# Twenty products instead of 24 for one half of one group's w_in product, and an earlier place for that half's weight sums

## The chip, the cores and the metric

The kernel runs on one core of a Trainium2 chip. The metric is the device time of one execution in microseconds (us), lower is better. A median of three runs is given for the kernel before. Engine names are those of the profile: PE is the matrix engine, PEld its weight load, DVE the vector engine, ACT the scalar engine, POOL the general engine, SP the engine that issues most transfers.

## The reference: what is computed

Two blocks follow each other. The first is a gated linear attention over 4 batches, 8 heads, 768 positions and a head width of 48. The second is a two-layer network on its result, laid out as 3072 rows of 384 numbers.

```
state = alpha[t] * state + outer(k[t], v[t])     # 48 x 48 for every batch and head
y[t]  = q[t] @ state
x = y as (batch * position, head * width)        # 3072 x 384
h = x @ w_in                                     # w_in 384 x 2048
g = h / (1 + exp(-h))                            # silu
out = g @ w_out                                  # w_out 2048 x 384
```

All of it is in 32-bit floating point; `w_in` and `w_out` come in as 64-bit numbers and are converted on the chip.

## The kernel before, in words

`quotients` is the function that runs; `general`, a slower fallback, stands behind a flag and isn't run on these inputs.

**Attention.** The 3072 rows are 24 chunks of 128 rows (`NT`, line 402). A chunk's attention is spread over two steps of the main loop (line 1185), each step with four slots. `products` (line 698) and `quotient` (line 742) are DVE work: transposes of alpha, k and q, two scans, and the products kp (lines 737 and 739) and p (line 758). In the next step come `scores` (line 780: PE multiplies p by kp, ACT copies the result, POOL masks it), `values` (line 831: PE, then an ACT copy into `xt`) and `states` (line 853: PE, and a DVE addition at line 868). `flip` (line 760) turns kp for the state by way of memory. So PE cannot start the scores of a chunk before DVE has written that chunk's p.

**Network.** Four chunks are a group, so there are 6 groups; a group has two halves of 256 rows. `enter_plain` (line 897) computes `x @ w_in` for one half of the rows and eight of the sixteen 128-column blocks of `w_in` (a `pair`), in four pieces; a piece is six matrix products of 128x256 on PE, and one silu on ACT. `enter` (line 917) computes the same for both halves of the rows together with a scheme of fast matrix multiplication: 20 products in seven pieces, where the plain way takes 24 for the same outputs. Each product is two matrix products of 128x256 (line 929). The scheme needs sums of blocks of `w_in` (`sums_w`, line 589, 23 DVE operations for a pair, from the table at line 335), sums of blocks of the rows (`sums_x`, line 878, 11 DVE operations, line 343), and for each call 12 ACT copies out of PSUM (line 936), 13 DVE additions or subtractions (line 944), one more at line 998, and four silus (line 941) that follow those additions. `sums_w` writes some of its results over `w_in` itself, so no plain product may use that pair of columns afterwards. `leave` (line 1021) computes `g @ w_out` for half a group, with seven products in seven pieces (a scheme of the same kind), and DVE additions at lines 1033, 1042, 1074, 1076 and 1085. `side_by_side` (line 1016) is one DVE addition that `leave` needs.

**Which groups use which.** Group 0 and group 1 are computed by `enter_plain`; groups 2 to 5 by `enter`. The sums of `w_in` for pair 0 are made during `leave(0, 1)`, those for pair 1 during `leave(1, 0)` (line 1050, function `done`).

**Order.** The pieces of the network stand in one list, `pieces` (line 1120), each with a weight of 12 and with the number of chunks that must have been through `values` before it. `both` (line 1116) takes two lists alternately. `fill` (line 1166) is called at the end of every slot and takes so many pieces as are due: within a phase (`phases`, line 1125; `marks`, line 1152) the work is spread evenly over the slots. The second phase, the one with group 1's later parts, runs from slot 35 to slot 50, four slots to a step. Its list before is

```
pieces += [plain(1, 1, 0)] * 4
both([(leave(0, 1), 12, GB)] * 7, [plain(1, 0, 1)] * 4 + [plain(1, 1, 1)] * 4)
```

PE's instructions keep the order in which the program traces them once `late` is filled (`settle`, line 1154, at slot 31). DVE's order is made by the framework's list scheduler when the program is built, apart from the sums (lines 582 to 587), which keep their order among themselves (line 594). [...]

`late` holds the buffers that are allocated at slot 31 over the space of the start-up buffers: `wx` for the sums of `w_in`, `xc` for the sums of rows (one buffer, line 879), `part` (one buffer) for `enter`, `turn` (one buffer) for the transposed k and q.

Of the kernel before, what the change touches and what calls it, by code (L numbers as in the profile page):

```python
# [355 lines left out]
def quotients(  # L356
# [22 lines left out]
    late = {}  # L379
# [25 lines left out]
    GB = 4  # L405
# [183 lines left out]
    def sums_w(pair, upto):  # L589

        r = slice(2 * pair, 2 * pair + 2)
        while sums_done[pair] < min(upto, len(SUMS_W)):
            to, sa, a, sb, b = SUMS_W[sums_done[pair]]
            tc.keep_in_program_order(
                combine(block_w(to)[:, r], sa, block_w(a)[:, r], sb, block_w(b)[:, r]))
            sums_done[pair] += 1

    sums_done = [0] * (NQ // 2)

    def differences(i):  # L600

        if i < HF // 2:
            i = slice(2 * i, 2 * i + 2)
            tc.keep_in_program_order(
                dve.tensor_tensor(t1[:, i], b12[:, i], b11[:, i], ALU.subtract))
            dve.tensor_tensor(t2[:, i], b22[:, i], t1[:, i], ALU.subtract)
            dve.tensor_tensor(t4[:, i], b21[:, i], t2[:, i], ALU.subtract)
        else:
            i -= HF // 2
            side_by_side(0, i % 2, i // 2)  # L610
            i = slice(2 * i, 2 * i + 2)
            dve.tensor_tensor(b12[:, i], b22[:, i], b12[:, i], ALU.subtract)
# [275 lines left out]
    def g_tiles(grp, pair):  # L888
        for h in range(2):
            gts[grp, h, pair] = gpool.tile([128, 4, 2, TB], F32, name="g")  # L890
# [6 lines left out]
    def enter_plain(grp, h, pair):  # L897

        if h == 0:
            g_tiles(grp, pair)  # L900
        xt = xts[2 * grp + h]
        for f in range(8 * pair, 8 * pair + 8, 2):
            ps = bank(f // 2 % 3).rearrange("p (e n) -> p e n", e=2)
            for e in range(2):
                for t in range(NKT):
                    pe.matmul(ps[:, e, :], lhsT=w_in[:, t, (f + e) * 128 : (f + e + 1) * 128],
                              rhs=xt[:, t, :], start=(t == 0), stop=(t == NKT - 1))
            q, i = divmod(f, 4)
            act.activation(gts[grp, h, pair][:, i : i + 2, q % 2, :], ps, AF.Silu)  # L909
            if grp == 1 and pair == h == 0:  # L910
                differences(f // 2)
                differences(4 + f // 2)
            if grp > 0 and f % 8 == 6:
                side_by_side(grp, h, pair)
            yield

    def enter(grp, pair):
        g_tiles(grp, pair)
        halves = [gts[grp, h, pair] for h in range(2)]

        s = [halves[o % 2][:, o // 2] for o in range(8)]
        todo = iter(PRODUCTS)

        def new(i):
            return bank(i).rearrange("p (e n) -> p e n", e=2)

        def add(ps, first=False):
            w, x = next(todo)
            for e in range(2):
                pe.matmul(ps[:, e], lhsT=block_w(w)[:, 2 * pair + e], rhs=block_x(grp, x),  # L930
                          start=(first and e == 0), stop=(e == 1), skip_group_check=True)

        def copy(ps, to=None):
            if to is None:
                to = late["part"].tile([128, 2, TB], F32, name="part")
            act.copy(to, ps)  # L936
            return to

        def silu(h, i):
            x = halves[h][:, i : i + 2]  # L940
            act.activation(x, x, AF.Silu)  # L941

        def tt(to, a, b, op=ALU.add):
            dve.tensor_tensor(to, a, b, op)  # L944

        a, b, c = [new(i) for i in range(3)]
        add(a, True)
        copy(a, s[6])
        add(b, True)
        copy(b, s[2])  # L950
        add(c, True)
        tt(s[6], s[6], copy(c), ALU.subtract)
        yield
        add(a)
        t = copy(a)
        add(b)
        copy(b, s[4])
        add(c)
        copy(c, s[7])
        tt(s[7], s[7], t, ALU.subtract)  # L960
        yield
        add(a)
        copy(a, s[5])
        add(b)
        copy(b, s[3])
        tt(s[5], s[5], s[3])
        add(c)
        copy(c, s[0])
        yield
        add(a)  # L970
        tt(s[4], a, s[4])
        b = new(1)
        add(b, True)
        add(b)
        copy(b, s[1])
        yield
        c = new(2)
        add(c, True)
        tt(s[2], s[2], copy(c), ALU.subtract)
        a = new(0)  # L980
        add(a, True)
        tt(s[6], a, s[6])
        silu(0, 2)
        add(b)
        tt(s[5], copy(b), s[5], ALU.subtract)
        yield
        add(c)
        tt(s[1], c, s[1])
        tt(s[3], s[1], s[3], ALU.subtract)
        a = new(0)  # L990
        add(a, True)
        tt(s[2], a, s[2])
        add(b)
        tt(s[7], b, s[7])
        silu(1, 2)
        yield
        add(c)
        combine(s[1], -1, s[1], -1, s[0])
        tt(s[0], c, s[0])
        silu(0, 0)  # L1000
        a = new(0)
        add(a, True)
        tt(s[3], a, s[3])
        silu(1, 0)
        turn.append(turn.pop(0))
        for h in range(2):
            side_by_side(grp, h, pair)
        yield
# [12 lines left out]
    def leave(grp, h):  # L1021


        def product(ps, m, k, w, first=False):
            for i in range(HF):
                q = i // 2
                x = gts[grp, h, q // 2][:, 2 * (i % 2) + k, q % 2, m * C : (m + 1) * C]
                pe.matmul(ps, lhsT=x, rhs=w[:, i], start=(first and i == 0), stop=(i == HF - 1),
                          skip_group_check=True)

        def subtract(to, x, y):
            for pair in range(NQ // 2):
                dve.tensor_tensor(cells(grp, h, pair, *to), cells(grp, h, pair, *x),  # L1033
                                  cells(grp, h, pair, *y), ALU.subtract)

        def store(m, c, x, y=None):
            ci, b = divmod(GB * grp + 2 * h + m, B)
            o = opool.tile([128, HO], F32, name="o")
            if y is None:
                act.copy(o, x)  # L1040
            else:
                dve.tensor_tensor(o, x, y, ALU.add)  # L1042
            r = b * S + ci * C

            (gps if grp < NG - 1 else nc.sync).dma_start(out[r : r + C, c * HO : (c + 1) * HO], o)  # L1045

        u1, u2, u3, u4 = [rpool.tile([128, HO], F32, name=f"u{j}") for j in range(4)]
        steps = iter(range(7))

        def done():  # L1050
            if 2 * grp + h in (1, 2):
                sums_w(2 * grp + h - 1, 4 * next(steps) + 4)

        def new(i):
            return out_bank(i, HO)

        a, b = new(0), new(1)
        product(a, 0, 0, b11, True)
        act.copy(u1, a)
        subtract((0, 0), (1, 0), (0, 0))  # L1060
        done()
        yield
        product(b, 1, 0, t1, True)
        act.copy(u4, b)  # L1064
        done()
        yield
        product(a, 0, 1, b21)
        store(0, 0, a)
        subtract((0, 1), (0, 1), (0, 0))
        done()  # L1070
        yield
        b = new(1)
        product(b, 0, 0, t2, True)
        dve.tensor_tensor(u2, b, u1, ALU.add)
        subtract((1, 0), (1, 1), (0, 0))
        dve.tensor_tensor(u2, u2, u4, ALU.add)
        done()
        yield
        a = new(0)
        product(a, 0, 1, b22, True)  # L1080
        store(0, 1, a, u2)
        done()
        yield
        product(b, 1, 0, b12)
        dve.tensor_tensor(u3, b, u1, ALU.add)
        store(1, 1, u3, u4)
        done()
        yield
        a = new(0)
        product(a, 1, 1, t4, True)  # L1090
        store(1, 0, a, u3)
        done()
        yield
# [13 lines left out]
    def plain(grp, h, pair):  # L1107
        return (enter_plain(grp, h, pair), 12, 2 * (2 * grp + h) + 2)

    def group(grp):  # L1110
        return [[(enter(grp, pair), 12, GB * grp + GB)] * 7 for pair in range(2)]

    def output(grp):
        return [[(leave(grp, h), 12, GB * grp + GB)] * 7 for h in range(2)]
# [1 line left out]
    def both(x, y):  # L1116
        for i in range(max(len(x), len(y))):
            pieces.extend(x[i : i + 1] + y[i : i + 1])

    pieces = []  # L1120
# [3 lines left out]
    pieces += [plain(1, 0, 0)] * 4 + [(leave(0, 0), 12, GB)] * 7  # L1124
    phases = [len(pieces)]
    pieces += [plain(1, 1, 0)] * 4
    both([(leave(0, 1), 12, GB)] * 7, [plain(1, 0, 1)] * 4 + [plain(1, 1, 1)] * 4)
    phases.append(len(pieces))
    before = output(1)
    for grp in range(2, NG):  # L1130
# [168 lines left out]
```

## Time and profile before

| what | value |
|---|---|
| median of 3 runs | 561.26 us (560.49 to 562.18) |
| span of the profiled execution, first to last instruction | 558.1 us |
| median less span (what lies around it) | 3.2 us |
| PE busy | 541.4 us, 97% of the span |
| PEld busy | 488.8 us, 88% |
| DVE busy | 445.1 us, 80% |
| ACT busy | 208.4 us, 37% |
| POOL busy | 75.9 us, 14% |
| mean granted PE clock | 0.994 |

For the profiled execution only its span is given, and no device time of its own, so what lies around the span is taken from the median of the runs. A row of a timeline gives the start, the time from the first start to the last end of the instructions it merges, the engine, the line, the output and the inputs, and a number of instructions; a bracket gives the idle time of the engine ahead of it and what ended it. A matrix product in 32 bits appears as two MATMUL records. Matrix products overlap in PE's pipeline, so the distance between starts, not the length of one record, is what each costs on PE.

### The profile page before, as it was taken

To read this page: it belongs to the slowest core of one execution; us is meant where nothing else is said; L and a number is where in the kernel's file an instruction comes from. 1 tells how busy PE (TensorE), PEld (TensorE's weight loads), DVE (VectorE), ACT (ScalarE), POOL (GpSimd) and SP (SyncE) were. 2 spreads that over 40 slices of the span, in tenths; PEclk is the share of its full clock that TensorE was granted. 3 is DMA by queue.
4 is the path that set the end of the run, shared out by engine and by line. 5 is a ranking of instruction groups with operands and counts; after the bars stand their busy time and mean duration, and the time that the engine had idled before them with its cause. 6 is when DMAs were issued, how large, how long until landed. Compare 5 with 4: busy or idle time off the path is not lost. (4 is left out here: it accounts for less than half of the span.)

```text
span 558.1 us, 12640 instructions
## 1 busy us (share of the span) xinstructions
PE 541.4 (97%) x5026; PEld 488.8 (88%) x5026; DVE 445.1 (80%) x801; ACT 208.4 (37%) x466; POOL 75.9 (14%) x146
## 2 busy tenths in 40 slices
PE   5999999999999999999999999999999999999996
PEld 3788887998899898899999999988998999998996
DVE  5887889974999799997998986998894775857531
ACT  3456643223333243353353353353263341432200
POOL 4100010221211211021021021021121000001000
PEclk9799999999999999999999999999999999999999
DMA  9999861164445525355445654717712122333101
GB/s 218 255 276 177 232 189 40 38 164 108 126 131 136 142 62 134 88 145 157 129 109 142 194 141 115 198 22 179 180 48 84 53 99 95 111 109 106 38 25 32
DMA packets 99220, 70.13 MB, mean 126 GB/s; under 512 B 56272, under 2 KB 88656, under 8 KB 99152
## 3 DMA queue, kind: packets, MB, share of 16 engines
q1 hardware_dynamic: 97232, 65.30, 44.6%
q0 software_dynamic: 1920, 3.93, 2.0%
q8 instruction: 41, 0.67, 0.5%
q14 instruction: 27, 0.22, 0.1%
HBM read 61.34 MB, written 7.86 MB: 124 GB/s over the span
## 5 line engine op out<-in xcount | busy, mean ns | idle before, releaser
L388 PE MATMUL ps_o<-w_out,g 128*128 128x192 f32 x768 | 134.7, 329 | 1.1 <-DVE o L1042 0.9
L388 PEld LDWEIGHTS ps_o<-w_out,g 128*128 128x128 f32 x768 | 125.4, 190 | 5.1 <-DVE o L1042 2.3
L388 PE MATMUL ps_m<-xt,w_in 128*128 128x256 f32 x480 | 113.6, 383 | 1.5 <-ACT xt L851 1.1
L388 PEld LDWEIGHTS ps_m<-xt,w_in 128*128 128x128 f32 x480 | 89.1, 190 | 14.4 <-ACT xt L851 1.6
L388 PE MATMUL ps_o<-wt,g 128*128 128x192 f32 x576 | 99.7, 326 | 0.0
L388 PEld LDWEIGHTS ps_o<-wt,g 128*128 128x128 f32 x576 | 95.1, 190 | 1.6 <-issue 0.2
L388 PE MATMUL ps_m<-xc,w_in 128*128 128x256 f32 x288 | 70.7, 382 | 0.0
L685 DVE TENSOR_REDUCE seen<-bits 128x1 f32<-128x384 int32 (+2 forms) x65 | 42.5, 689 | 24.0 <-DMA bits<-in_moe_w_out_dram 19.6
L388 PEld LDWEIGHTS ps_m<-xc,w_in 128*128 128x128 f32 x288 | 53.6, 190 | 7.0 <-DVE g L944 0.3
L941 ACT ACTIVATE g<-g 128x1024 f32<-128x1024 f32 x32 | 33.0, 1056 | 59.0 <-DVE g L944 59.0
L1033 DVE TENSOR_TENSOR g<-g 128x512 f32<-128x512 f32 x72 | 49.8, 708 | 6.1 <-PE ps_o L388 6.1
L1045 POOL DMA_DIRECT2D out_dram<-o x40 | 22.0, 550 | 223.2 <-DVE o L1042 127.6
L813 POOL TENSOR_SCALAR_AFFINE_SELECT g<-g 64x256 f32<-64x256 f32 x64 | 34.2, 534 | 124.8 <-ACT g L806 105.8
L388 PE MATMUL ps_m<-xc,wx 128*128 128x256 f32 x192 | 50.0, 383 | 1.0 <-DVE xc L586 1.0
L936 ACT COPY g<-ps_m 128x512 f32<-128x512 f32 x64 | 36.5, 588 | 36.5 <-PE ps_m L388 36.4
L388 PEld LDWEIGHTS ps_m<-xc,wx 128*128 128x128 f32 x192 | 35.2, 190 | 5.3 <-ACT u L1064 1.3
L944 DVE TENSOR_TENSOR g<-ps_m,g 128x512 f32<-128x512 f32 x56 | 37.0, 684 | 2.9 <-PE ps_m L388 2.7
L722 DVE TENSOR_TENSOR_SCAN u<-al,one 128x516 f32<-128x516 f32 x24 | 30.0, 1249 | 10.6 <-ACT al L719 10.3
L909 ACT ACTIVATE g<-ps_m 128x512 f32<-128x512 f32 x32 | 19.1, 596 | 42.8 <-PE ps_m L388 42.3
L936 ACT COPY part<-ps_m 128x512 f32<-128x512 f32 x32 | 18.9, 589 | 43.0 <-DVE g L944 21.3
L752 DVE TENSOR_TENSOR_SCAN p<-al,inv 128x516 f32<-128x516 f32 x24 | 29.9, 1246 | 1.0 <-PE ps_a L388 0.4
L388 PE MATMUL ps_a<-g,vn 128*32 128x128 f32 x768 | 27.5, 278 | 1.8 <-POOL g L801 1.7
(126 smaller groups left out, 611.4 us busy)
## 6 DMA issues: line engine op xcount, KB each, us to landing
bits<-in_moe_w_in_dram SPq DMA_DIRECT2D x24, 512.0 KB, 4.8
bits<-in_moe_w_out_dram SPq DMA_DIRECT2D x32, 384.0 KB, 3.1
at<-in_alpha_dram SPq DMA_DIRECT2D x64, 96.0 KB, 2.5
kt<-in_k_dram SPq DMA_DIRECT2D x64, 96.0 KB, 2.5
qt<-in_q_dram SPq DMA_DIRECT2D x64, 96.0 KB, 2.6
bits<-in_alpha_dram SPq DMA_DIRECT2D x9, 512.0 KB, 3.8
out_dram<-o POOLq DMA_DIRECT2D x40, 96.0 KB, 2.4
flips<-turn SPq DMA_DIRECT2D x12, 256.0 KB, 2.4
```

The source lines that it names most:

```text
L388: in_order(nc.tensor.matmul(*args, **kw))
L685: dve.tensor_reduce(seen[kind][which][:, i : i + 1], x, axis=AX, op=op, apply_absolute_value=True))
L722: dve.tensor_tensor_scan(u[:, end - 1 :: -1], sg[:, end:0:-1], one[:, end:0:-1], 0.0, ALU.mult, ALU.add)
L752: dve.tensor_tensor_scan(p[:, 0:end], sg[:, 0:end], iv[:, 0:end], 0.0, ALU.mult, ALU.add)
L813: gps.affine_select(x, x, pattern=[[0, NP], [1, CH]], compare_op=ALU.is_ge, fill=0.0, base=0, channel_multiplier=-1)
L909: act.activation(gts[grp, h, pair][:, i : i + 2, q % 2, :], ps, AF.Silu)
L936: act.copy(to, ps)
L941: act.activation(x, x, AF.Silu)
L944: dve.tensor_tensor(to, a, b, op)
L1033: dve.tensor_tensor(cells(grp, h, pair, *to), cells(grp, h, pair, *x), cells(grp, h, pair, *y), ALU.subtract)
L1045: (gps if grp < NG - 1 else nc.sync).dma_start(out[r : r + C, c * HO : (c + 1) * HO], o)
```

## The change

Group 1's second pair of columns no longer goes through `enter_plain` for each half (two times four pieces) but through one `enter(1, 1)` (seven pieces, `second(1, 1)`). Its sums of the rows, `sums_x(1)`, are put ahead of it in the list, after the four pieces of `plain(1, 1, 0)`. The sums of `w_in` for pair 1 are made from `leave(0, 0)`, three for each of its pieces that come once `late` is filled, and from the pieces of `plain(1, 1, 0)`, four each; `enter` makes what is then missing at its start. They are no longer made in `leave(1, 0)`. The second phase thus holds 18 pieces of weight 12 and one of weight nought instead of 19 of weight 12. Groups 0 and 2 to 5, and pair 0 of group 1, are computed as before.

```diff
@@ enter_plain
             if grp == 1 and pair == h == 0:
                 differences(f // 2)
                 differences(4 + f // 2)
+            if grp == h == 1:
+                sums_w(1, sums_done[1] + 4)
             if grp > 0 and f % 8 == 6:
                 side_by_side(grp, h, pair)
             yield
@@
     def enter(grp, pair):
+        sums_w(pair, len(SUMS_W))
         g_tiles(grp, pair)
@@ leave
         def done():
-            if 2 * grp + h in (1, 2):
-                sums_w(2 * grp + h - 1, 4 * next(steps) + 4)
+            if grp == h == 0 and late:
+                sums_w(1, sums_done[1] + 3)
+            if grp == 0 and h == 1:
+                sums_w(0, 4 * next(steps) + 4)
@@
+    def second(grp, pair):
+        return [(enter(grp, pair), 12, GB * grp + GB)] * 7
+
     def group(grp):
-        return [[(enter(grp, pair), 12, GB * grp + GB)] * 7 for pair in range(2)]
+        return [second(grp, pair) for pair in range(2)]
@@
     pieces += [plain(1, 1, 0)] * 4
-    both([(leave(0, 1), 12, GB)] * 7, [plain(1, 0, 1)] * 4 + [plain(1, 1, 1)] * 4)
+    pieces.append((sums_x(1), 0, 2 * GB))
+    both([(leave(0, 1), 12, GB)] * 7, second(1, 1))
```

## Prediction

> **What bounds the kernel now.** I read the page's busy times first, then the busy times of the stretches around the change, then what PE and DVE waited for there, then the two engines' timelines. The page:
>
> ```profile
> PE 541.4 (97%) x5026; PEld 488.8 (88%) x5026; DVE 445.1 (80%) x801; ACT 208.4 (37%) x466; POOL 75.9 (14%) x146
> ...
> PE   5999999999999999999999999999999999999996
> ...
> DVE  5887889974999799997998986998894775857531
> ```
>
> PE bounds the kernel over the whole span; it idles only at the two ends. DVE averages 80%, but it has slices of 9 next to slices of 4, and an average says nothing of the stretch that changes. So I cut that stretch at PE's own marks: 101.9 us (first piece of leave(0, 0)), 126.9 us (plain(1, 1, 0) begins), 192.4 us (last product of the second phase, one piece of leave(1, 0) and the scores after it), 236.5 us. The columns are length, then busy time of PE, PEld, DVE, ACT and POOL with counts.
>
> ```profile
> 101.90:126.90 25.00, 24.77 (x310) 23.18 (x308) 20.36 (x36) 4.53 (x12) 6.34 (x11) 1.00 0.44 116
> 126.90:192.40 65.50, 64.99 (x752) 58.43 (x752) 53.34 (x96) 20.27 (x59) 10.81 (x20) 1.00 0.48 128
> 192.40:236.50 44.10, 42.75 (x434) 38.37 (x432) 43.50 (x84) 17.54 (x41) 6.21 (x12) 1.00 0.36 96
> ```
>
> Call them A, B and C. DVE has 4.6 us free in A, 12.2 us in B and 0.6 us in C, where it is as full as PE and PE loses 1.35 us. The waits and the timelines say who is late:
>
> ```profile
> DVE g L1019 <- ACT g L909: 10.1, 2, 7.6
> ...
> PE ps_m L388 <- DVE g L944: 1.3, 2, 0.9
> ...
> PE ps_a L388 <- DVE p L758: 0.5, 1, 0.5
> ```
>
> ```profile
> 139.25 0.69 DVE L1019 TENSOR_TENSOR g<-g 128x512 f32<-128x512 f32 x1 [7.62 <-ACT g L909]
> ...
> 143.87 0.90 PE L388 MATMUL ps_a<-p,kp 48*64 48x128 f32 x32 [0.48 <-DVE p L758]
> ...
> 144.70 2.86 PE L388 MATMUL ps_m<-xt,w_in 128*128 128x256 f32 x12
> ...
> 147.40 2.76 PE L388 MATMUL ps_o<-wt,g 128*128 128x192 f32 x16
> ...
> 150.00 2.75 PE L388 MATMUL ps_m<-xt,w_in 128*128 128x256 f32 x12
> ...
> 158.55 0.69 DVE L758 TENSOR_TENSOR p<-turn,p 128x512 f32<-128x512 f32 x1
> ...
> 160.07 0.90 PE L388 MATMUL ps_a<-p,kp 48*64 48x128 f32 x32
> ```
>
> Of B's 12.2 free us, 7.6 lie in one place, before the side-by-side sum at 139.25 us, which waits for the end of plain(1, 1, 0). From 139.25 to 192.4 us DVE has no hole but 0.41 and 2.49 us. And there it runs just in time: p is written at 143.7 us and PE, which had waited 0.48 us, starts the scores at 143.87; the next p ends at 159.24 for scores at 160.07. Its lead is about 1 us. B's second part is bounded by PE with DVE a hair behind.
>
> [...] here a record of 128x256 is 379 to 383 ns long, while a piece of 12 such records holds PE for 2.59 us (it starts at 150.00, and the next work on PE starts at 152.59), 216 ns each. I use 216. [...] The trace has 418 and 684. [...] here starts lie 0.34 to 0.45 us apart for the 0.42 us sums and 0.60 for the 0.68 ones, so the trace decides and I count distances.
>
> **The change part by part.**
>
> PE. Plain: 2 x 4 pieces x 6 products x 2 records = 96 records. Enter: 20 x 2 x 2 = 80. So 16 x 0.216 = **3.46 us** less, all of it on the path, in B, at the end of the interleaved list (the seventh piece has 2 products, the eighth is gone). PE's need in B becomes 64.99 - 3.46 = 61.5 us. If nothing else changed, this alone gives 557.8.
>
> DVE, added to B: enter's 14 additions on 128x512 at 0.60 us = 8.4 us; sums_x(1), 11 on 128x256. Those of group 2 took from 190.39 to 196.53 with 1.35 us of other work between, 0.435 each; eight sums of w_in took 150.69 to 153.74, 0.38 each. I take 0.40: 4.4 us. The two side-by-side sums stay. Together **12.8 us**.
>
> DVE, moved: 23 sums for pair 1 at 0.38 = 8.7 us leave C. By the slots, late is filled after the third piece of leave(0, 0), so four of its pieces make 12 (4.6 us, in A) and plain(1, 1, 0) makes the other 11 (4.2 us, in B). They issue no transfer and pass neither SP's nor POOL's queue. In A the cover is DVE's idle time, 2.96 us after 113 us (1.49, 0.23, 0.89, 0.35), so DVE slips by about 2 us; p there ends at 125.7 us for scores at 129.71, so PE loses nothing; without that cover it would be up to 0.6 us. In B the cover is the 7.6 us hole: 2 + 4.2 fit. Cost at PE nought; left of the hole 1.4 us. Their memory, wx, lies over start-up buffers whose last readers are done by about 114 us.
>
> ACT gets 12 copies at 0.59 and 4 silus at 1.06 and loses 8 silus at 0.60: +6.5 us on 20.3 of 65.5. Hidden by its idle time; but silus of enter wait for DVE, and what is behind them on ACT waits too. What stands behind sums_x on DVE is the rest of its queue: the transposes of k and q, p, and through p PE's scores; the SP loads of the next k and q follow those transposes. xc has one buffer, so sums_x(2) now waits for enter(1, 1)'s 19th product; that is so between all later groups (275 to 285 us) and PE shows no loss over 0.3 us there.
>
> The ledger, DVE against PE:
>
> - A: DVE 20.4 + 4.6 = 25.0; PE 24.8.
> - B: DVE 53.3 + 4.2 + 12.8 = 70.3; PE 61.5.
> - C: DVE 43.5 - 8.7 = 34.8; PE 42.75.
>
> A and B together need 95.3 us of DVE and 86.3 us of PE; before they took 90.5. So **DVE becomes the bound of B**. With no hole at all it ends B 4.8 us later than before. Two unknowns shift that. What DVE may leave behind for C: the last addition, two side-by-side sums, a flip and the 2 us of sums_x(2) that lay before 192.4, at most 0.6 + 1.2 + 0.65 + 2 = 4.4 us; at least nothing, since the first piece of leave(1, 0) needs enter's last sums and silus and the scores need p. I take 2.4. And the holes DVE will keep: the 1.4 us left before 139.25 and about 1 us in A at least, 4 us if ACT and DVE wait for each other as in C; I take 2.4. The two cancel: B ends 4.8 us later. In C DVE then has 8 us to spare, so its two late additions should vanish: -1.3 us. What was lost by PE in B does not come back, since PE bounds C. Sum: +4.8 - 1.3 = **+3.5 us**: span 561.6, plus 3.2 around it, 564.8. The same difference stands against the median of the runs, 561.26. Both ends: 4.8 - 4.4 + 1 - 1.3 = +0.1, and 4.8 - 0 + 4 - 1.3 = +7.5.
>
> **The rivals.**
>
> R1, PE takes what it is given: the scheduler lets p and enter's bank reads pass and puts the sums where DVE leads (the pair-0 sums are done at 180.4 us and needed at 193.3, so 13 us of lead exist), and the lag runs into C's 8 us of room. Then B is PE's: -3.46, and C gives up to -1.35: 556.4 to 557.8, say 557.3. For it: C's DVE room is nearly the 8.8 us overload of B. Against: before, those sums were not put late, and the lead of p was 1 us. It decides if DVE can be 9 us behind without p being behind.
>
> R2, about no change: sums_x is pulled into the hole and the lag of 4.4 us is fully allowed: 559.6 to 563.
>
> R3, worse: enter's chain of bank, DVE addition, silu and bank again stalls in itself while DVE is late, and each late p adds: 4 us more of holes than assumed, 568 to 572.
>
> That the sums come too late (if late were filled only after leave(0, 0)) would put up to 7 further sums, 2.7 us, ahead of enter: it lies within the range.
>
> **How the numbers follow.** Runs spread about 0.3%, 1.7 us, which is what a measurement can tell from no change. Likeliest, DVE bounds B: 0.60, 563 to 568.5, at 564.8. R1 0.18 (556.4 to 559.6, as some lag may be felt). R2 0.16. R3 0.06. Slower by over 0.3% (above 562.9): 0.60 + 0.06 = 0.66. Within: 0.16. Faster (below 559.6): 0.18. The range goes from 558.0, which leaves out some 0.12 of R1, to 569, which leaves out nearly all of R3: 0.17 together.
>
> **What would show it.** Right: DVE without holes from about 140 us to the end of the second phase; waits of PE's scores for p (L758), or of PE for additions of enter or silus, adding up to 7 to 9 us between 140 and 200 us; no wait for L944 in leave(1, 0)'s stretch; 96 records become 80. Wrong: PE without waits there, the second phase 3 us shorter, and sums of w_in or rows lying late without harm. The prediction fails if DVE work of B turns out not to be on p's way, or if distances in enter are much under 0.60 us.

## The result and the profile after

The changed kernel takes **568.28 us** (median of 4 runs, 567.9 to 568.67) against 560.97 us (4 runs, 560.49 to 562.18) on the same chip. The ratio is 1.0127, with a 95% interval of 1.0115 to 1.014: it is 7.3 us slower, twice the forecast of 3.5, and near the upper end of the range (558 to 569). The span of its profiled execution is 566.1 us, 8.0 us more than before; that execution took 567.96 us as a whole. So 1.9 us lie around its span, and 1.7 to 1.9 in nearly every execution that has both numbers, not the 3.2 us that the table of the kernel before gives: its profiled execution of 558.1 us thus took about 559.9 us (an estimate), less than any of its four timed ones, and the 8.0 us are somewhat more than the medians' 7.3.

The page of the changed kernel (line numbers beyond 911 have moved by 3: L1019 is now L1022, L944 is L947, L1042 is L1045):

```profile
PE 542.3 (96%) x5010; PEld 488.4 (86%) x5010; DVE 455.3 (80%) x826; ACT 214.5 (38%) x474; POOL 76.4 (13%) x146
...
PE   6999999999889989999999999999999999999996
...
DVE  5897789988999998887998987998884775857531
...
PEclk9999999999989999999999999999999999999999
```

PE has 16 records fewer, as many as forecast, and yet is busy for longer, and there are now 8s in PE's row: it waits in the middle of the kernel. DVE has 25 more instructions and 10.2 us more work. The third thing to see is one slice in the middle, from 156 to 170 us, in which the granted PE clock is 8 tenths. The kernel before has only a slow slice near its start:

```profile
PEclk9799999999999999999999999999999999999999
```

The stretches B and C of the prediction, cut at the same times, with columns as before (length, busy time of PE, PEld, DVE, ACT, POOL, then the granted clock):

```profile
126.90:192.40 65.50, 58.87 (x631) 52.25 (x632) 61.72 (x120) 22.54 (x65) 12.14 (x22) 0.97 0.45 118
192.40:236.50 44.10, 41.99 (x429) 37.88 (x428) 39.69 (x71) 18.68 (x42) 6.01 (x12) 1.00 0.44 115
```

B has turned round: DVE is busy for 61.72 of 65.5 us and PE for 58.87, where before it was 53.34 and 64.99. The waits from 126.9 to 242 us:

```profile
PE ps_a L388 <- DVE p L758: 5.6, 3, 2.4
...
DVE g L1022 <- ACT g L909: 2.6, 1, 2.6
...
PE ps_m L388 <- DVE g L947: 0.9, 2, 0.5
```

DVE's hole ahead of the side-by-side sum has shrunk from 7.6 to 2.6 us, and PE now waits three times for p. PE's timeline, with some of its rows:

```profile
145.34 0.90 PE L388 MATMUL ps_a<-p,kp 48*64 48x128 f32 x32 [1.80 <-DVE p L758]
...
148.86 2.76 PE L388 MATMUL ps_o<-wt,g 128*128 128x192 f32 x16
151.46 1.03 PE L388 MATMUL ps_m<-xc,wx 128*128 128x256 f32 x4
...
164.02 0.90 PE L388 MATMUL ps_a<-p,kp 48*64 48x128 f32 x32 [2.41 <-DVE p L758]
164.85 4.55 PE L388 MATMUL ps_o<-wt,g 128*128 128x192 f32 x16
169.24 1.03 PE L388 MATMUL ps_m<-xc,wx 128*128 128x256 f32 x4
...
180.73 0.90 PE L388 MATMUL ps_a<-p,kp 48*64 48x128 f32 x32 [1.35 <-DVE p L758]
...
198.15 1.43 PE L388 MATMUL ps_a<-p,kp 48*64 48x128 f32 x32
...
206.84 1.10 PE L388 MATMUL ps_m<-xc,wx 128*128 128x256 f32 x4 [1.54 <-DVE inv L750]
```

Three things are to be read here. The sixteen w_out records at 148.86 hold PE for 2.60 us (the next work starts at 151.46); the same sixteen at 164.85, just after the wait of 2.41 us, hold it for 4.39. The wait at 206.84 is for a sum of the rows: the releaser named, a reciprocal, ends just before (206.78), but the product reads `xc`. By the tables from line 343 on this product takes the eighth row sum, which DVE ends at 206.69 (206.27 and 0.42 in the timeline under e9), 0.15 us ahead of the product, the same distance as from p's end to the scores. And the scores at 198.15 last 1.43 us instead of 0.90: their weight loads wait 0.35 us for an ACT copy (L851), which stood behind one of the last silus of `enter(1, 1)`.

**Where the 8.0 us lie.** The scores recur in every step, so their starts on PE are marks that stand in any version. I name those of before S1 (129.71 us), S5 (192.49), S7 (236.59) and the last scores (426.03). S1 to S5 is nearly B, S5 to S7 is nearly C.

| stretch | before | after | difference |
|---|---|---|---|
| start to S1 | 129.71 | 129.86 | +0.15 |
| S1 to S5 | 62.78 | 68.29 | +5.51 |
| S5 to S7 | 44.10 | 44.57 | +0.47 |
| S7 to the last scores | 189.44 | 189.65 | +0.21 |
| the last scores to PE's last w_out piece | 124.70 | 126.16 | +1.46 |
| rest | 7.37 | 7.57 | +0.20 |

### The profile page after: what moved, and what is told of

It is laid out like the page before. It is cut to its first block, busy times and chain, and to the rows that moved or that the text cites. A ratio compares the mean times of both kernels' runs of the same rounds, so it can differ in the third digit from the quotient of the medians.

```text
span 566.1 us, 12639 instructions
## 1 busy us (share of the span) xinstructions
PE 542.3 (96%) x5010; PEld 488.4 (86%) x5010; DVE 455.3 (80%) x826; ACT 214.5 (38%) x474; POOL 76.4 (13%) x146
## 5 line engine op out<-in xcount | busy, mean ns | idle before, releaser
L388 PE MATMUL ps_m<-xt,w_in 128*128 128x256 f32 x396 | 94.7, 383 | 1.5 <-ACT xt L851 1.1
L388 PEld LDWEIGHTS ps_m<-xt,w_in 128*128 128x128 f32 x396 | 73.4, 190 | 12.8 <-ACT xt L851 1.6
L388 PE MATMUL ps_m<-xc,w_in 128*128 128x256 f32 x324 | 79.7, 382 | 0.3 <-DVE xc L582 0.3
L388 PEld LDWEIGHTS ps_m<-xc,w_in 128*128 128x128 f32 x324 | 60.3, 190 | 8.1 <-DVE xc L582 0.4
L685 DVE TENSOR_REDUCE seen<-bits 128x1 f32<-128x384 int32 (+2 forms) x65 | 42.5, 687 | 28.1 <-DMA bits<-in_moe_w_out_dram 23.1
L944 ACT ACTIVATE g<-g 128x1024 f32<-128x1024 f32 x36 | 37.3, 1056 | 64.9 <-DVE g L947 64.8
L388 PE MATMUL ps_m<-xc,wx 128*128 128x256 f32 x216 | 56.4, 383 | 2.6 <-DVE inv L750 1.5
L939 ACT COPY g<-ps_m 128x512 f32<-128x512 f32 x72 | 41.1, 588 | 42.1 <-PE ps_m L388 41.8
L947 DVE TENSOR_TENSOR g<-ps_m,g 128x512 f32<-128x512 f32 x63 | 41.6, 680 | 2.9 <-PE ps_m L388 2.7
L388 PEld LDWEIGHTS ps_a<-p,kp 48*64 48x64 f32 (+1 forms) x640 | 21.3, 149 | 12.9 <-issue 9.7
L388 PE MATMUL ps_a<-p,kp 48*64 48x64 f32 (+2 forms) x640 | 25.6, 262 | 5.7 <-DVE p L758 5.6
```

The source lines that it names most:

```text
L388: in_order(nc.tensor.matmul(*args, **kw))
L685: dve.tensor_reduce(seen[kind][which][:, i : i + 1], x, axis=AX, op=op, apply_absolute_value=True))
```

## The experiments

**Theory:** DVE has too much to do between 127 and 200 us, above all ahead of the first p after its hole; PE waits for p, and the 3.46 us that PE saves can't be had. **Rivals:** the early sums of `w_in` are what costs, not the twenty products; `enter(1, 1)` has a cost of its own on PE or in its chain of copy, addition and silu; the one buffer of `xc` holds back the next group's row sums; PE's clock, not DVE, makes the time. All runs are in one table; the ratio is to the kernel before on the same chip, and the two stretches are from each kernel's own profile, which is one execution (before 62.78 and 44.10).

| kernel | median us | before | ratio (95%) | S1 to S5 | S5 to S7 |
|---|---|---|---|---|---|
| changed kernel | 568.28 | 560.97 | 1.0127 (1.0115 to 1.0140) | 68.29 | 44.57 |
| e1_move_only | 559.42 | 560.90 | 0.9977 (0.9966 to 0.9987) | 63.43 | 41.94 |
| e2_no_sums_w0 | 564.43 | 560.90 | 1.0066 (1.0041 to 1.0091) | 64.27 | 44.62 |
| e3_rows_first | 564.47 | 560.90 | 1.0068 (1.0044 to 1.0092) | 65.22 | 44.63 |
| e4_no_sums_x1 | 563.48 | 560.90 | 1.0047 (1.0032 to 1.0062) | 64.13 | 44.67 |
| e5_busy_wait | 565.34 | 560.51 | 1.0088 (1.0074 to 1.0102) | 68.21 | 42.64 |
| e9_no_sums_x2 | 564.82 | 560.51 | 1.0087 (1.0073 to 1.0101) | 69.33 | 41.94 |
| e7_pool_x | 566.42 | 560.51 | 1.0107 (1.0092 to 1.0123) | 66.81 | 44.64 |
| e7_pool_xw | 570.85 | 560.51 | 1.0182 (1.0165 to 1.0199) | 70.31 | 44.60 |
| e10_rows_first_no_w0 | 564.35 | 560.64 | 1.0064 (1.0046 to 1.0081) | 64.18 | 44.57 |
| e12_no_w_sums | 560.22 | 560.83 | 0.9988 (0.9979 to 0.9997) | 59.55 | 44.64 |
| e11_early_eight | 559.18 | 560.64 | 0.9975 (0.9965 to 0.9985) | 62.79 | 41.93 |
| e13_early_both | 559.65 | 560.83 | 0.9978 (0.9962 to 0.9993) | 63.32 | 41.94 |

From S7 to the last scores all of them take 189.4 to 190.0 us, so nothing of the change reaches into that part.

### e1_move_only: the early sums alone

The kernel before, with the sums for pair 1 made early and the plain products kept.

```diff
@@ enter_plain
+            if grp == h == 1 and pair == 0:
+                sums_w(1, sums_done[1] + 4)
@@ leave, done()
-            if 2 * grp + h in (1, 2):
-                sums_w(2 * grp + h - 1, 4 * next(steps) + 4)
+            if grp == h == 0 and late:
+                sums_w(1, sums_done[1] + 3)
+            if grp == 0 and h == 1:
+                sums_w(0, 4 * next(steps) + 4)
```

> The kernel before with only the earlier place of the 23 sums of w_in for pair 1; group 1 still takes 24 products (so its second pair of columns is computed from blocks already overwritten by sums, and rows 512 to 1023 in the kernel's order come out other than the reference's). Theory (DVE is the bound of the second phase because of what enter(1, 1) adds to it): DVE holds 12 sums in the first stretch and 11 in the hole ahead of the side-by-side sum, PE loses nothing there, and the third stretch loses its two waits for L944: 559.0 to 560.5 us, 0.5 to 2 us under before. Rival (the earlier sums are what costs, by delaying p and the stores of leave(0, 0)): 563 us or more.

It came to 559.42 us. PE's only wait in B is 1.14 us for the first p instead of 0.48, and the stretch S5 to S7 falls from 44.10 to 41.94 us: the two waits for L944 are gone. So moving the sums alone isn't what costs; it gains 1.5 us, and the loss of the changed kernel belongs to `enter(1, 1)` or to the two together.

### e2, e3 and e4: one load taken off DVE at a time

e2_no_sums_w0 takes out the 23 sums of pair 0, which lie in B:

```diff
@@ enter
-        sums_w(pair, len(SUMS_W))
+        if pair == 1:
+            sums_w(pair, len(SUMS_W))
@@ leave, done()
-            if grp == 0 and h == 1:
-                sums_w(0, 4 * next(steps) + 4)
@@ where late is filled
+        gps.memset(late["wx"][:, :, 0:2], 0.0)
```

> The changed kernel without the 23 sums of w_in for pair 0 (the blocks that they would write are zeroed once or left raw, so groups 2 to 5 come out other than the reference's). It takes 8.7 us of DVE work out of the second phase that has nothing to do with enter(1, 1). Theory (load on DVE, whatever it consists of): DVE's need in the second phase falls from 70.3 to 61.6 us, PE's is 61.5, so PE's waits for p fall from 5.6 us to under 2 us, and the time to 557.5 to 561 us. Rival (the chain of bank, addition and silu within enter(1, 1), or the single xc buffer, makes the loss): 565 to 568 us.

It came to 564.43, between the two. The trace says why: there is now one wait for p in B, for the first one (3.52 us, at 147.10), and none after it. With 8.7 us of DVE work gone the later waits vanish, but the first grows, since the built order of DVE has other work ahead of that p: seven row sums and three sums of `w_in` after the side-by-side sum (the text on e10 below counts twelve row sums there, but there are only eleven in all).

e3_rows_first puts the row sums of group 1 ahead of `plain(1, 1, 0)` in the list:

```diff
-    pieces += [plain(1, 1, 0)] * 4
     pieces.append((sums_x(1), 0, 2 * GB))
+    pieces += [plain(1, 1, 0)] * 4
```

> The changed kernel with sums_x(1) ahead of the four pieces of plain(1, 1, 0) in the list instead of behind them. Theory: the 11 sums can fall into the 2.6 us hole that DVE keeps before the side-by-side sum, and no longer stand before the first p of the second phase; the wait of 1.8 us for that p shrinks, and at most 2.6 us are won: 565.7 to 567.5 us. Rival (the place of these sums doesn't matter because PE's loss comes later in the phase): 568 to 568.5 us.

564.47: it gained 3.8 us on the changed kernel (3.3 by the ratios), more than the 0.8 to 2.6 forecast. DVE has no hole any more between 126 and 147 us. But the reason given was wrong: the wait for the first p did not shrink, it grew from 1.80 to 2.21 us. The gain came behind it, where a single wait of 2.01 us was left: DVE did 2.6 us of its work in what had been a hole, and the rest of B had that much less to do.

e4_no_sums_x1 takes those eleven sums out:

```diff
@@ sums_x
+        if grp == 1:
+            gps.memset(xcs[grp], 0.0)
+            yield
+            return
```

> The changed kernel without the 11 sums of the rows of group 1 (POOL zeroes the tile instead, so rows 512 to 1023 in the kernel's order come out other than the reference's). It takes 4.4 us from DVE in the second phase. Theory: PE wins back nearly all of that, and perhaps the slow matrix products after its longest wait: 562.5 to 565 us. Rival (loss by the single xc buffer before group 2's sums): no more than 1 us under the changed kernel, 567 us or more.

563.48, as the theory said; two waits for p are left, 1.13 us for the first one, ahead of which three row sums no longer stand, and 2.02 us for a later one. Eleven sums, 4.4 us of DVE, are worth 4.2 us of S1 to S5 (68.29 to 64.13). That is what a stretch bounded by DVE looks like.

### e5_busy_wait: is it the clock?

Sixteen w_out records took 4.39 us instead of 2.60 after the wait of 2.41 us. The granted clock in windows of 2 us shows it (the number behind POOL's count, ahead of the DMA share; changed kernel):

```profile
164.00:166.00 2.00, 1.98 (x38) 1.92 (x39) 2.00 (x5) 0.96 (x5) 0.20 (x1) 0.92 0.76 198
166.00:168.00 2.00, 2.00 (x8) 2.00 (x7) 1.96 (x6) 1.59 (x6) 1.80 (x4) 0.50 0.52 94
168.00:170.00 2.00, 2.00 (x9) 1.92 (x9) 1.97 (x4) 0.00 (x0) 0.02 (x1) 0.73 0.43 147
```

The clock was 0.92, 0.50 and 0.73, and 1.00 from 170 us on: 2 us x (0.08 + 0.50 + 0.27) = 1.7 us of PE's time lost, over some 3.4 us at half speed. It fell 1.6 us after the end of a wait of 2.41 us. To see what it costs, nine idle products of 128 columns, whose result is overwritten, stand ahead of these scores:

```diff
@@ scores
+        for _ in range(9 if n == 10 else 0):
+            pe.matmul(ps[0][:, 0, :], lhsT=ident, rhs=wt[:, 0, 0, 0:C], start=True, stop=True)
```

> The changed kernel with nine products of 128 columns put on PE ahead of the third scores of the second phase, where PE idled for 2.41 us and then ran a piece of 16 records in 4.4 instead of 2.6 us at a granted clock of 0.5. They need nothing that is late, their result is overwritten, and they last about 2 us at full clock, so they lie in the wait. Theory (the wait itself costs a second time, since the clock falls to half after it): the granted clock stays at 1.0 there and about 1.7 us are won: 566 to 567 us. Rival (the piece was slow for another reason, or the clock falls by the time of day and not by the wait): 568 us or more.

PE's timeline of this kernel:

```profile
163.03 0.90 PE L388 MATMUL ps_a<-p,kp 48*64 48x128 f32 x32 [0.36 <-DVE p L758]
163.86 2.87 PE L388 MATMUL ps_o<-wt,g 128*128 128x192 f32 x16
166.56 1.03 PE L388 MATMUL ps_m<-xc,wx 128*128 128x256 f32 x4
```

The drop is gone: the sixteen records hold PE for 2.70 us and the clock stays at 1.00. The kernel is about 2 us better (ratio 1.0088 against 1.0127), and at first that looks like the 1.7 us of the clock. The table says otherwise. S1 to S5 takes 68.21 us, as long as in the changed kernel (68.29): what PE no longer lost to its clock it lost to later waits for DVE (1.71 and 1.16 us for p, 1.18 for an addition of `enter`). The gain is in S5 to S7, 42.64 instead of 44.57, where DVE's order, built anew, has the row sums of group 2 earlier (0.62 us after S5 instead of 1.25). DVE's order within B changed too, but not its work, and it has no hole there in either kernel. So **the half clock wasn't the bound of the changed kernel's B; DVE was.**

### e9_no_sums_x2: the row sums of the next group

As e4, with `grp == 2`.

> The changed kernel without the 11 sums of the rows of group 2 (POOL zeroes the tile, so the rows of group 2 come out other than the reference's). The third stretch was forecast 1.3 us shorter and came out 0.5 us longer, with a wait of 1.5 us of PE for a sum of these rows. Theory (these sums stand late in DVE's queue because enter(1, 1)'s last additions stand ahead of them): the third stretch gets 2 to 2.7 us shorter, 565.5 to 566.5 us. Rival (the loss there comes from the chain of additions and silus that leave(1, 0) waits for): 567.5 to 568.5 us.

It came to 564.82, a little under the forecast. S5 to S7 falls to 41.94 us, 2.6 below the changed kernel and just what e1 has. This is C's relief, and with the row sums of group 2 it is lost: the two waits for them, 0.26 and 1.54 us, make 2.1 of the 2.6 with their breaks. The other 0.5 us is the stall within the scores at S5, which e9 doesn't have either: there ACT ends the last silu of `enter(1, 1)` 0.9 us ahead of S5, in the changed kernel (198.13) only with it. B isn't better (69.33): the clock was at 0.50 twice, for 3.4 us after a wait of 1.80 us and for 6.8 us around the end of one of 3.02 us. DVE's timeline of the changed kernel shows where those sums stand:

```profile
196.97 0.66 DVE L758 TENSOR_TENSOR p<-turn,p 128x512 f32<-128x512 f32 x1
197.56 1.30 DVE L1022 TENSOR_TENSOR g<-g 128x512 f32<-128x512 f32 x2
198.77 0.70 DVE L768 STREAM_TRANSPOSE turn<-kp 128x512 f32<-128x512 f32 x1
199.40 0.72 DVE L582 TENSOR_TENSOR xc<-xt 128x256 f32<-128x256 f32 x2
...
206.27 0.42 DVE L586 TENSOR_TENSOR xc<-xc,xt 128x256 f32<-128x256 f32 x1
206.61 0.17 DVE L750 RECIPROCAL inv<-least 128x4 f32<-128x4 f32 x1
```

They start at 199.40, 1.25 us after S5 (198.15). In the kernel before they start 2.1 us ahead of S5 (192.49):

```profile
189.03 0.68 DVE L758 TENSOR_TENSOR p<-turn,p 128x512 f32<-128x512 f32 x1
...
190.39 1.05 DVE L582 TENSOR_TENSOR xc<-xt 128x256 f32<-128x256 f32 x3
```

In both they follow p at a few places' distance in DVE's queue. But before, p was done 2.8 us ahead of its scores, and now it is done just in time, and these sums are late with it: they start 2.43 us after p does, where the kernel before has 1.36. Was it the buffer? The last product of `enter(1, 1)` that reads `xc` starts at 190.28 and is over by 191.5, 8 us before the first of these sums, and DVE is not idle in between: it is the work ahead of them on DVE that holds them, not the buffer. Whether the single buffer made the scheduler place them that late isn't shown; no version with two buffers was run.

### e7_pool_x and e7_pool_xw: the sums on POOL

POOL is busy for 13% of the span. e7_pool_x puts ten of the eleven row sums of group 1 there, e7_pool_xw also 21 of the 23 sums of `w_in` for pair 1; the scaled additions at line 587 stay on DVE.

```diff
-    def combine(to, sa, a, sb, b):
+    def combine(to, sa, a, sb, b, on=nc.vector):
         if sa == sb == 1:
-            return dve.tensor_tensor(to, a, b, ALU.add)
+            return on.tensor_tensor(to, a, b, ALU.add)
...
@@ sums_x
-                combine(block_x(grp, to), sa, block_x(grp, a), sb, block_x(grp, b)))
+                combine(block_x(grp, to), sa, block_x(grp, a), sb, block_x(grp, b),
+                        gps if grp == 1 else dve))
```

> The changed kernel with ten of the eleven sums of the rows of group 1 on POOL, which is 14% busy, instead of DVE (the eleventh, with two minus signs, stays on DVE). Theory: DVE gets 4 us less in the second phase; PE gains as much as by leaving these sums out, less what DVE's operations lose while POOL works (in the kernel before, DVE operations of 0.55 us took 0.87 and 0.98 while POOL masked scores): 563.5 to 566 us. Rival (POOL is too slow or stands behind its own waits, and PE then waits for these sums): 567 us or more.

> As the kernel with the sums of rows on POOL, and 21 of the 23 sums of w_in for pair 1 on POOL too, where they have from 114 to 144 us. Theory: DVE gets 8 us less in the first two stretches, about its whole overload, and PE's 3.46 us come through in part: 559.5 to 563.5 us. Rival (POOL's work slows DVE as much as it relieves it, or POOL is late): 564 us or more.

566.42 and 570.85: the first gained less than hoped (0.2% in ratio), the second lost, and for it the rival was right. DVE's and PE's timelines of e7_pool_xw (its numbers beyond line 595 are up by one):

```profile
134.23 0.60 DVE L587 SCALAR_TENSOR_TENSOR w_in<-wx,w_in 128x256 f32<-128x256 f32 x1 [3.90 <-POOL w_in L582]
...
145.76 0.43 DVE L587 SCALAR_TENSOR_TENSOR xc<-xt,xc 128x256 f32<-128x256 f32 x1 [4.97 <-POOL xc L582]
...
147.29 0.79 DVE L738 TENSOR_TENSOR kp<-turn,u 128x256 f32<-128x256 f32 x1
148.00 0.94 DVE L740 TENSOR_TENSOR kp<-turn,u 128x256 f32<-128x256 f32 x1
...
150.94 1.56 PE L388 MATMUL ps_a<-p,kp 48*64 48x128 f32 x32 [6.71 <-DVE p L759]
```

Most sums take 0.73 us on POOL, some up to 1.7, where DVE needs 0.42. The few that stay on DVE waited there for POOL, two of them 3.90 and 4.97 us. DVE did not pass over these two: the transposes of k and q and p stood behind the second one until it was through, and PE waited 6.71 us for that p. And DVE's own products kp, which ran while POOL made sums (147.07 to 149.53 us), took 0.79 and 0.94 us, where the two at 194.16 and 194.48 us of the changed kernel, with POOL making none, took 0.42 and 0.43. What slowed them isn't shown.

### e10 and e12: no sums of w_in

e10_rows_first_no_w0 joins e2 and e3.

> The changed kernel with both edits of the earlier runs: sums_x(1) ahead of plain(1, 1, 0), and the 23 sums of w_in for pair 0 left out (groups 2 to 5 come out other than the reference's). Leaving out those sums alone won only 3.9 us, because PE then waited 3.5 us for the first p of the phase and ran 1.7 us slow after it; in the trace 12 sums of rows stood ahead of that p. Theory (DVE's load and the place of its work together make the whole loss): with both mended PE's waits in the second phase fall under 1.5 us, no slow clock, and the 3.46 us of PE come through: 558 to 560.5 us. Rival (enter(1, 1) has a cost of its own on PE, by its banks or silus): 562 us or more.

The forecast missed: 564.35, no better than either. PE's timeline has one wait for p in B, and after it the clock drops:

```profile
146.35 0.90 PE L388 MATMUL ps_a<-p,kp 48*64 48x128 f32 x32 [3.43 <-DVE p L758]
```

```profile
148.00:150.00 2.00, 2.00 (x6) 1.55 (x6) 1.97 (x2) 1.93 (x10) 1.73 (x3) 0.50 0.66 144
```

DVE is full from 126 to 147 us: the 23 sums of pair 1 and the eleven row sums are all queued by then, about 13 us of work, where the kernel before had 2.96 us idle in A after 113 us and the hole of 7.62. So the load in front of the **first** p was still there, and taking work out behind it couldn't help. From the next scores after S1 (S2, at 143.87 us in the kernel before) to S5, e10 takes 47.07 us, where the kernel before takes 48.62.

e12_no_w_sums tests that reading: as e3, and without any of the 46 sums.

```diff
@@ enter_plain
-            if grp == h == 1:
-                sums_w(1, sums_done[1] + 4)
@@ enter
-        sums_w(pair, len(SUMS_W))
@@ leave, done()
-            if grp == h == 0 and late:
-                sums_w(1, sums_done[1] + 3)
-            if grp == 0 and h == 1:
-                sums_w(0, 4 * next(steps) + 4)
@@ where late is filled
+        gps.memset(late["wx"], 0.0)
```

> The changed kernel with the sums of the rows of group 1 ahead of plain(1, 1, 0), and without any of the 46 sums of w_in: both pairs' columns of wx are zeroed once by POOL instead, so products that use them are of zeros, and the others use w_in as it came. It takes some 17.6 us of DVE work (46 at 0.38) out of the stretches A and B. Theory, the loss comes from what stands on DVE ahead of the first p after the side-by-side sum: with 13 us of sums there reduced to the 11 sums of rows (4.4 us), that first p isn't waited for by more than 0.5 us, PE's granted clock stays at 1.00 through B, the 3.46 us of PE come through whole, and C keeps the loss that stands with sums_x(2) behind enter(1, 1) (0.5 to 2 us over the kernel before): 557.5 to 559.5. Rival, enter(1, 1) has a cost of its own on PE or in its chain of copy, addition and silu that no sum of w_in explains: 562 or more, with PE waits inside B after the first p.

PE's timeline:

```profile
143.67 0.90 PE L388 MATMUL ps_a<-p,kp 48*64 48x128 f32 x32 [0.49 <-DVE p L758]
...
189.06 1.47 PE L388 MATMUL ps_a<-p,kp 48*64 48x128 f32 x32
...
197.82 1.10 PE L388 MATMUL ps_m<-xc,wx 128*128 128x256 f32 x4 [1.57 <-DVE inv L750]
```

In B it is as the theory said: one wait of 0.49 us, as in the kernel before, the clock at 1.00, and S1 to S5 takes 59.55 us instead of 62.78, so 3.2 of the 3.46 us come through. In B `enter(1, 1)` has no other cost of its own that shows; there that rival is out. From S2 to S5 e12 takes 45.39 us and e10 47.07; neither waits for DVE in between, and the 1.7 us are the half clock of e10. There it did count, since DVE was not behind. In S5 to S7 e12 has nearly the 44.57 us of the changed kernel (44.64), the same wait for the rows (1.57 us) and the same slow scores (1.47), though DVE carries none of the moved load: what is late in C is late by its place, behind p and the last additions of `enter(1, 1)`. The time as a whole, 560.22, is above the 557.5 to 559.5 that was expected: by the last scores e12 is 2.6 us ahead of the kernel before, and in the end part it gives 2.0 of them back (126.70 us against 124.70).

### e11 and e13: what the change had right

e11_early_eight is the kernel before, with only those eight sums of pair 1 early that write nothing but `wx`, so the plain products stay as they are.

```diff
@@ leave, done()
+            if grp == h == 0 and late:
+                sums_w(1, min(sums_done[1] + 3, 8))
+            if grp == 0 and h == 1:
+                sums_w(0, 4 * next(steps) + 4)
+            if grp == 1 and h == 0:
+                sums_w(1, 8 + 15 * (next(steps) + 1) // 7)
```

> The kernel before, computing all that the reference does, with only those eight sums of w_in for pair 1 made early (in leave(0, 0), as in the change) that write to wx and not over w_in; the other 15 are made in leave(1, 0) as before, and group 1 takes 24 products. Theory (the third stretch lacks a little of DVE, its two waits for L944 are 1.35 us): a third of the load that the whole move took from it is enough for a part of those: 559.5 to 560.5 us against 561 before, and not above it. Rival (the gain of the whole move came from elsewhere): 560.5 to 561.5 us.

559.18, 0.25% below the kernel before: S5 to S7 takes 41.93 us, without waits, and B is untouched (62.79). Of the kernels that compute everything this has the lowest ratio, though e13 lies within its interval. e13_early_both does the same for pair 0 too, from the pieces of `plain(1, 1, 0)`:

```diff
@@ enter_plain, on top of e11
+            if grp == h == 1 and pair == 0:
+                sums_w(0, min(sums_done[0] + 2, 8))
```

> The kernel before with the eight sums of w_in of each pair that write only to wx made early: those of pair 1 from leave(0, 0), as in the run with the early eight, and those of pair 0 from the four pieces of plain(1, 1, 0), two each, where DVE has its hole of 7.6 us; the other 15 of each pair stay where they were. The whole computation is kept. Theory: B was bounded by PE with waits of 0.5 us and p only about 1 us ahead, so eight sums (3 us) fewer on DVE between 139 and 192 us can win at most those 0.5 us; C is that of the early eight alone: 558.6 to 559.3. Rival: the sums are traced ahead of the k, q transposes in plain(1, 1, 0) and delay the first p after the hole as in the changed kernel: 559.5 to 561.

559.65: no further gain, and inside the rival's range. The wait for the first p went from 0.48 to 1.02 us: with more sums ahead of it a little of the rival came true, in spite of the hole.

## Why the prediction was half right

**PE's saving: right.** 3.46 us were to be saved in B; e12 shows 3.2 when nothing stands in the way. The distances between starts by which the prediction counted are what the traces have: on PE, records of 128x256 that last 379 to 383 ns start 216 ns apart; on DVE, sums of 256 columns that last 418 ns start 0.34 to 0.45 us apart, and additions of 512 columns that last 684 ns 0.60 us apart.

**The moved sums: nearly right.** They were to cost PE nothing; alone (e1) they cost 0.7 us at the first p, 1.14 instead of 0.48 us of waiting, and won three times as much in C. The count was off: in the changed kernel nine of them lie in A and not twelve, since the first starts at 119.66 us and not at 113; eleven come until 135.2, and three stand after DVE's hole.

**DVE bounds B, and B ends 4.8 us later: right, 5.5 measured.** From the side-by-side sum at 139.40 to beyond S5 DVE shows no hole. PE's side of the same 5.5: waits of 1.80, 2.41, 1.35, 0.50, 0.40 and 0.20, together 6.66 instead of 0.48; about 0.15 more for each of five more breaks, as a bracket counts from the end of the last product, which lies beyond the point where the next would start (an estimate: a record of 128x256 lasts 0.38 us and the next starts after 0.22); 1.7 us of half clock; less the 3.46: 5.2. The hole kept 2.6 us, not 1.4, because of the order. DVE's timeline right after it, where the kernel before has nothing but the two transposes and kp ahead of p:

```profile
139.40 0.69 DVE L1022 TENSOR_TENSOR g<-g 128x512 f32<-128x512 f32 x1 [2.63 <-ACT g L909]
140.00 0.75 DVE L582 TENSOR_TENSOR xc<-xt 128x256 f32<-128x256 f32 x2
140.68 1.11 DVE L696 STREAM_TRANSPOSE turn<-kt 128x512 f32<-128x512 f32 x1
141.63 0.41 DVE L582 TENSOR_TENSOR xc<-xt 128x256 f32<-128x256 f32 x1
...
142.62 0.40 DVE L586 TENSOR_TENSOR w_in<-w_in 128x256 f32<-128x256 f32 x1
142.94 0.41 DVE L582 TENSOR_TENSOR w_in<-wx 128x256 f32<-128x256 f32 x1
143.28 1.07 DVE L696 STREAM_TRANSPOSE turn<-qt 128x512 f32<-128x512 f32 x1
144.20 0.40 DVE L582 TENSOR_TENSOR w_in<-wx,w_in 128x256 f32<-128x256 f32 x1
144.53 0.67 DVE L758 TENSOR_TENSOR p<-turn,p 128x512 f32<-128x512 f32 x1
```

Three row sums and three leftover sums of `w_in`, some 2.1 us, stand among the transposes and kp that p needs, right behind 2.63 us in which DVE did nothing. With the row sums gone (e4) the wait for this p is 1.13 us instead of 1.80, and with neither kind behind the hole (e12) it is 0.49. e3 filled the hole and gained 3.8 us, though behind the first p. The ledger by stretch couldn't see this: it counted work against time over 65 us, where the first p, 18 us into it, is the first to feel what stands ahead of it.

**C gives back 1.3 us: wrong, and this is the step that failed.** The two late additions did vanish, as forecast, and without the row sums of group 2 in the way that is worth 2.2 us (e1, e9, e11, e13: 41.93 to 41.94 us). But S5 to S7 became 0.5 us longer. The prediction had written "What DVE may leave behind for C" into the ledger as relief for B, and put 2 us of `sums_x(2)` into it, and held of `xc` that "PE shows no loss over 0.3 us there". What was left behind was all eleven sums, and PE waited for them in C (0.26 and 1.54 us); 0.5 us more went into the slow scores at S5. Work pushed over a border isn't free if the next stretch begins by needing it. Between forecast and profile, 3.5 and 8.0 us, this is 1.8 us of the 4.5. And the profile of the kernel before had the warning. The prediction read `xc` at the entry of group 3 (275 to 285 us) and said that it is so "between all later groups". At the entry of group 4 PE waits for a row sum, at the very product that it waits for in C of the changed kernel:

```profile
369.77 1.10 PE L388 MATMUL ps_m<-xc,wx 128*128 128x256 f32 x4 [1.02 <-DVE xc L586]
```

**The rest.** B accounts for 0.7 us more, the start, the part from S7 to the last scores and the tail together for 0.6. The last 125 us of the kernel account for 1.5 in the profiles, and were in no step. So the two larger misses, in C and at the end, went the same way and make most of the doubling; that 568.28 is still inside the range comes from the width given to other unknowns, not from a sum that held. In those last 125 us DVE waits for transfers at the reading of `w_out`'s 64-bit numbers (L685); two lines of the waits after 424 us, of the kernel before:

```profile
DVE seen L685 <- DMA bits<-in_moe_w_out_dram: 19.6, 14, 2.5
...
PE ps_o L388 <- DVE o L1042: 0.9, 2, 0.7
```

and of the changed one:

```profile
DVE seen L685 <- DMA bits<-in_moe_w_out_dram: 23.1, 14, 2.9
...
PE ps_o L388 <- DVE o L1045: 2.4, 3, 1.2
```

The two additions that PE waited longest for in the changed kernel (0.95 and 1.25 us) start at 486.06 and 523.07 us, behind one of these readings each (484.54 and 521.55, 1.00 us). How much of PE's waiting comes from the earlier waits for transfers isn't shown. The same stretch takes 126.0 us in e11, 126.7 in e12 and 128.9 in e1, so its length isn't set by the change alone; the profile of before, with 124.7, is the shortest of all fourteen. How much of it the change itself costs stays open. It is also the part in which e12 gave back most of its lead, as far as its one profile shows.

**The signs named ahead.** The waits between 140 and 200 us were to add up to 7 to 9 us, and added up to 6.9. No wait for the additions in `leave(1, 0)`'s stretch: so it was, but a wait for the rows stood in its place. R3, with 568 to 572, had the size right by another way: not a chain of `enter` that stalls in itself (e12 shows none in B), but the late rows and the end part.

## What to carry to other kernels

Make the ledger of an engine up to the first consumer that it feeds, not over the whole stage: free time counts only where the built order puts work into it, and work queued ahead of a result on the critical way delays it even beside an idle hole (here PE waited 1.80 us for a p with 2.1 us of sums ahead of it, behind a hole of 2.63 us, and 0.49 us in e12 without those sums there). When work is left behind for the next stage, ask what that stage needs first. And before the price of a slowed clock or a removed wait is booked, compare the same stretch between two marks in both versions: e5 looked like the clock and was the order. And when one border shows that a shared buffer or a late sum costs nothing, look at the other borders too before saying so of all.

## What the runs showed of the hardware that was not expected

In these runs the granted PE clock fell to half (0.50) after PE had waited for about 2 us, but the length of the wait alone doesn't decide. It fell soon after, or during the end of, waits of 1.80 us (e9), 2.01 (e3), 2.02 (e4), 2.41 (changed kernel), 3.02 (e9), 3.37 (e7_pool_x), 3.43 (e10), 3.52 (e2) and 6.71 us (e7_pool_xw). It didn't after 1.80 us in the changed kernel and in e5, nor after 2.21 us in e3:

```profile
143.46 0.90 PE L388 MATMUL ps_a<-p,kp 48*64 48x128 f32 x32 [1.80 <-DVE p L758]
```

```profile
145.05 0.90 PE L388 MATMUL ps_a<-p,kp 48*64 48x128 f32 x32 [2.21 <-DVE p L758]
```

The first is e9's, with the clock at half from 144.2 to 147.6 us, the second e3's, with the clock at 1.00 after it. The starts of the drops tell more, read from the clock in windows of 0.05 us. The drops seen last 3.4 us, or twice that (e9's second one, e7_pool_xw, and from 15.4 to 22.25 us in the kernel before). Within a trace the drops start whole steps of 3.413 us apart: e9's at 144.20 and 178.35 us, ten steps; e2's at 15.65 and 148.75, 39 steps; and the changed kernel's at 165.65 and at 565.0, where its work ends, 117 steps. An estimate from these starts: borders lie 3.413 us apart through the whole of a trace, and what counts is how much PE waits between two of them. Counted so, the step ahead of each of these drops holds 1.7 us of waiting or more (1.78 in the changed kernel, 1.76 in the kernel before), and no step with up to 1.6 us was followed by one. e3's 2.21 us fall on both sides of a border, 1.1 us each, and of the changed kernel's 1.80 us 1.6 lie in one step. One step of e2, with about 1.8 us, had no drop, nor had one at the start of the kernel before and of the changed one (from 1.8 us on, 2.3 and 2.4 us of waiting), so this count doesn't tell all of them apart. The estimate is worked out from the traces after the fact; no run was made to test it.

3.4 us at a clock of 0.50 are 1.7 us of PE's time. They told in the length of a stretch only where PE was its bound: 1.7 us between e10 and e12 (47.07 and 45.39 us from S2 to S5), and nothing in B of the changed kernel (68.29 us from S1 to S5, 68.21 in e5 without the drop).
